# Up to two of three exponent-bit shifts moved to GpSimd, with term-wise products and a packed output projection, in a fused attention kernel

## The chip, the cores and the metric

The kernel runs on one core of a Trainium2 chip, with one launch. The metric is device time in microseconds (us). The kernel before takes 801.9 us at the median of its first three runs (798.03 to 802.26). Each timed run also has the mean clock that TensorE was granted, as a share of full speed.

## The reference, cut to what matters

Two attention layers read separate inputs of 2048 rows and 512 columns, and their outputs are joined side by side.

```python
def _A_ref(x, wq, wk, wv, wo):           # H = 32 query heads, ONE key/value head, Dh = 16
    q = (x @ wq).reshape(B, S, H, Dh).transpose(0, 2, 1, 3)
    k, v = x @ wk, x @ wv
    scores = einsum("bhqd,bkd->bhqk", q, k) * Dh ** -0.5
    p = softmax(scores)                   # 32 x 2048 x 2048 exponentials
    o = einsum("bhqk,bkd->bhqd", p, v)
    return o.transpose(0, 2, 1, 3).reshape(B, S, H * Dh) @ wo

def _B_ref(x, wqkv, w_phi, wo):           # linear attention
    ...
    phi_q = concat([softmax(pq), softmax(-pq)])     # the same for phi_k
    kv, z = einsum("bhsf,bhsd->bhfd", phi_k, v), phi_k.sum(s)
    o = (phi_q @ kv) / (phi_q . z + 1e-6)
    return o.reshape(B, S, D) @ wo
return concatenate([a, b], axis=-1)
```

Part A costs most: 32 x 2048 x 2048, or 134 million, exponentials. Part B is dense matrix work, small beside it.

## The kernel before

The program is planned when it is built. A small list scheduler in Python gives each job (a few instructions on one engine) an estimated duration and picks the order; the chip then runs that fixed order with semaphores.

**Scores on TensorE, a quarter of the array at a time.** A head has 16 columns, so a score matmul contracts over at most 32 rows. Four of them run side by side, each in its own group of 32 rows ("row tiles"). The products with the values use 32 columns each, four side by side ("column tiles").

```python
def score(self, pe, bank, sc, kap, g):            # row tile g
    return pe.matmul(self.ps[:, bank, :], lhsT=self.KR[32*g:32*g+32, ...], rhs=self.QA[32*g:32*g+32, ...],
                     start=True, stop=True, tile_position=(32 * g, 0))

def pv(self, q):                                  # ScalarE's path: four column tiles
    ...
    for g in range(4):
        mm = pe.matmul(ps[32*g:32*g+32, bank, :], lhsT=w, rhs=PT[:, slots[g], :], start=start, stop=stop,
                       tile_position=(0, 32 * g))
```

**Exponentials on two engines.** ScalarE takes three or two banks of scores at a time from PSUM (the memory that matmuls write) and writes exp. VectorE takes the other tiles ("quads" of four) by building the bits of a half-precision float: `bits` evicts a score tile from PSUM as an int16 that is roughly 1024·log2(e)·score plus a bias. The exponential is then a weighted sum of four such floats, whose bits are shifted by 0, 256, 512 and 768. The three shifts are VectorE additions of a constant. The weights sit in the matmul's stationary operand (`VK`).

```python
def bits():                                       # four times a quad
    v.tensor_scalar(out=Z[:, 0, h, :], in0=ps[:, bank, :], scalar1=Z1, scalar2=Z0, op0=mult, op1=add)
def shift(t):                                     # t = 1, 2, 3: three times a quad
    v.tensor_scalar(out=Z[:, t], in0=Z[:, 0], scalar1=256.0 * t, scalar2=None, op0=add)

def d_pv(self, quad):                             # one job of 16 column-tiled matmuls
    for k in range(4):
        for g in range(4):
            mm = pe.matmul(ps[32*g:32*g+32, bank, :], lhsT=w[:, k, :], rhs=Zf[:, k, sl[g], :], ...)
```

**Few banks.** PSUM has eight banks: three and two for ScalarE's score groups, one for the accumulator, and two that the bit path and all of part B share (`self.free = [6, 7]`). TensorE runs its instructions in order, so a job that lacks a bank stops everything behind it.

**Fillers.** The planner keeps a running weight of TensorE's recent work over 3.41 us and inserts matmuls with no use (`fill`) when there is a gap and the weight is under `ACTIVE`.

```python
def weight(self, j):
    if k == "fill": return (j.dur / 0.2133) * (0.512 if j.mode == "full" else 0.25)
    if j.mode == "row": return 0.28 * (self.gsize[j.name[1]] if k == "qk" else 1)
    if j.mode == "col": return 0.41 if k == "kv" else 0.68 if k == "pv" else 2.7
    return dict(qs=0.13, q4=0.4, s6=0.8, wf=0.4).get(k, 2.4 * (j.dur - 0.02))
...
    if n >= 2 and te > 14 and self.active(s) < self.ACTIVE:     # ACTIVE = 6.4
        ... issue a fill
```

**Output projection.** Each of 31 blocks is normalised on VectorE into `On` (12 slots). The projection uses eight matmuls for 128 rows, with the weights padded by zeros (`wo_pad`, 8 slots), since only 16 of every 32 rows carry data.

## Time and profile before

| | before |
|---|---|
| time, first three runs | 801.9 us (798.03 to 802.26) |
| span of the profiled run, its granted clock | 800.5 us, 0.981 |
| busy: TensorE, VectorE, ScalarE, GpSimd | 754.1, 727.9, 746.9, 17.2 us |
| ScalarE idle (span less busy) | 53.6 us |

The first fence has lines of the profile page of the kernel before: busy time by engine (share of the span, number of instructions); the granted clock in 40 slices (9 means 90% or more); the engines' shares of the chain of waits that ended last; and the costliest groups (line, engine, operation, tiles, count, then busy us and mean ns, then idle time just before and its main releaser).

```profile
PE 754.1 (94%) x7457; PEld 246.6 (31%) x7457; DVE 727.9 (91%) x1261; ACT 746.9 (93%) x688; POOL 17.2 (2%) x49
...
PEclk9999999999799999999999999999899999999999
...
DVE 64%; PE 26%; ACT 4%; DMA 3%; SPq 2%; issue 1%; POOL 0%; DVEq 0%; POOLq 0%
...
L1645 ACT ACTIVATE f_PT<-f_ps 128x1536 bf16<-128x1536 f32 x619 | 719.5, 1262 | 36.4 <-PE f_ps L1590 33.0
L1737 DVE TENSOR_SCALAR f_Z<-f_ps 128x512 int16<-128x512 f32 x500 | 326.6, 681 | 28.5 <-PE f_ps L1590 28.1
L1590 PE MATMUL f_ps<-f_QA,f_KR 32*128 32x512 bf16 x2048 | 314.4, 389 | 24.2 <-DVE f_Z L1737 13.5
L1750 DVE TENSOR_SCALAR f_Z<-f_Z 128x2048 int16<-128x2048 int16 x375 | 247.8, 684 | 1.1
```

Three engines are over 90% busy. The chain says that VectorE ends last most often: L1737 are the evictions (`bits`), L1750 the shifts. ScalarE waits only 33 us in all for scores. TensorE's share of busy time has to be read with care, because ends of matmuls are modelled.

The table of stretches shows (columns: us, then busy us and instruction count of each engine, granted clock, share of the DMA engines, GB/s):

```profile
200.00:224.00 24.00, 23.47 (x201) 6.39 (x200) 21.39 (x38) 20.83 (x20) 0.00 (x0) 0.79 0.09 6
...
300.00:500.00 200.00, 191.23 (x1975) 64.75 (x1974) 183.53 (x316) 196.03 (x188) 5.35 (x10) 1.00 0.12 11
```

### The profile page before, as it was taken

To read this page: it belongs to the slowest core of one execution; us is meant where nothing else is said; L and a number is where in the kernel's file an instruction comes from. 1 tells how busy PE (TensorE), PEld (TensorE's weight loads), DVE (VectorE), ACT (ScalarE), POOL (GpSimd) and SP (SyncE) were. 2 spreads that over 40 slices of the span, in tenths; PEclk is the share of its full clock that TensorE was granted. 3 is DMA by queue.
4 is the path that set the end of the run, shared out by engine and by line. 5 is a ranking of instruction groups with operands and counts; after the bars stand their busy time and mean duration, and the time that the engine had idled before them with its cause. 6 is when DMAs were issued, how large, how long until landed. Compare 5 with 4: busy or idle time off the path is not lost.

```text
span 800.5 us, 17448 instructions
## 1 busy us (share of the span) xinstructions
PE 754.1 (94%) x7457; PEld 246.6 (31%) x7457; DVE 727.9 (91%) x1261; ACT 746.9 (93%) x688; POOL 17.2 (2%) x49
## 2 busy tenths in 40 slices
PE   8999999999999999999999999999999999989995
PEld 2323222333233233333333333333223333333332
DVE  3799999999899999997989898999899989999954
ACT  3999998999899999999999999999899999999972
POOL 5000000000000000011000000000000000000000
PEclk9999999999799999999999999999899999999999
DMA  6561111110111110111101111110111111011111
GB/s 133 111 129 9 9 7 8 8 8 4 6 8 21 22 8 4 7 9 8 9 4 19 35 7 9 21 15 10 6 9 21 22 21 19 11 9 15 21 14 37
DMA packets 45181, 17.12 MB, mean 21 GB/s; under 512 B 37092, under 2 KB 43236, under 8 KB 45096
## 3 DMA queue, kind: packets, MB, share of 16 engines
q1 hardware_dynamic: 45096, 15.93, 16.0%
q8 instruction: 60, 0.98, 0.5%
q14 instruction: 25, 0.20, 0.1%
HBM read 2.15 MB, written 4.19 MB: 8 GB/s over the span
## 4 chain that ended last, share of the span: by engine, by line
DVE 64%; PE 26%; ACT 4%; DMA 3%; SPq 2%; issue 1%; POOL 0%; DVEq 0%; POOLq 0%
DVE f_Z L1737 26%; DVE f_Z L1750 19%; PE f_ps L1590 8%; PE f_ps L1775 4%; PE f_ps L1687 4%; ACT f_PT L1645 4%; PE f_ps L2084 3%; DVE f_vS L2033 2%; DVE f_ssum L2007 2%; PE f_ps L1396 2%; DVE f_On L1818 2%; DVE f_Wk L2144 2%; DVE f_accS L1402 2%; PE f_ps L1831 1%; DMA f_denS<-f_denS 1%
## 5 line engine op out<-in xcount | busy, mean ns | idle before, releaser
L1645 ACT ACTIVATE f_PT<-f_ps 128x1536 bf16<-128x1536 f32 x619 | 719.5, 1262 | 36.4 <-PE f_ps L1590 33.0
L1737 DVE TENSOR_SCALAR f_Z<-f_ps 128x512 int16<-128x512 f32 x500 | 326.6, 681 | 28.5 <-PE f_ps L1590 28.1
L1590 PE MATMUL f_ps<-f_QA,f_KR 32*128 32x512 bf16 x2048 | 314.4, 389 | 24.2 <-DVE f_Z L1737 13.5
L1750 DVE TENSOR_SCALAR f_Z<-f_Z 128x2048 int16<-128x2048 int16 x375 | 247.8, 684 | 1.1
L1590 PEld LDWEIGHTS f_ps<-f_QA,f_KR 32*128 32x128 bf16 x2048 | 80.1, 91 | 256.0 <-ACT f_PT L1645 87.9
L1687 PE MATMUL f_ps<-f_PT,f_VA 128*32 128x512 bf16 x1548 | 152.5, 393 | 0.7 <-DVE f_accS L1402 0.2
L1775 PE MATMUL f_ps<-f_Z,f_VK 128*32 128x512 f16 x2000 | 133.3, 387 | 3.7 <-DVE f_Z L1750 1.7
L1396 PE MATMUL f_ps<-f_ones,f_zero 128*128 128x512 bf16 (+9 forms) x229 | 65.9, 354 | 2.0 <-POOL f_zero L1415 1.3
L1687 PEld LDWEIGHTS f_ps<-f_PT,f_VA 128*32 128x32 bf16 x1548 | 38.1, 93 | 93.5 <-issue 82.7
L1775 PEld LDWEIGHTS f_ps<-f_Z,f_VK 128*32 128x32 bf16 x2000 | 42.9, 96 | 64.5 <-DVE f_Z L1750 14.3
L2084 PE MATMUL f_ps<-f_BxT,f_Wq 128*128 128x512 bf16 x128 | 33.2, 382 | 1.6 <-DVE f_Z L1737 1.0
L1396 PEld LDWEIGHTS f_ps<-f_ones,f_zero 128*128 128x128 bf16 (+2 forms) x229 | 17.7, 97 | 33.2 <-issue 21.7
L1831 PE MATMUL f_ps<-f_wo_pad,f_On 128*128 128x512 bf16 x96 | 24.9, 382 | 0.6 <-DVE f_Z L1737 0.6
L2144 DVE TENSOR_TENSOR f_Wk<-f_ps,f_wq 128x512 bf16<-128x512 f32 x32 | 21.7, 681 | 2.7 <-PE f_ps L2133 2.7
L1818 DVE TENSOR_TENSOR f_On<-f_accS,f_denS 128x512 bf16<-128x512 f32 x31 | 21.2, 682 | 1.3 <-DMA f_denS<-f_denS 1.2
L1402 DVE COPY f_accS<-f_ps 128x512 f32<-128x512 f32 x31 | 21.2, 684 | 1.1 <-PE f_ps L1687 1.0
L2091 ACT ACTIVATE f_ET<-f_ps 128x512 bf16<-128x512 f32 x32 | 20.8, 649 | 0.6 <-PE f_ps L2084 0.5
L1542 DVE TENSOR_SCALAR f_KR<-f_ps,f_half 128x512 bf16<-128x512 f32 x8 | 5.6, 746 | 15.8 <-PE f_ps L1534 15.8
L2033 DVE TENSOR_TENSOR f_vS<-f_ps,f_rs 128x1024 bf16<-128x1024 f32 x16 | 19.6, 1222 | 0.0
L2001 ACT ACTIVATE f_Ek<-f_ps 128x512 bf16<-128x512 f32 x32 | 17.7, 622 | 1.8 <-PE f_ps L1993 1.7
L2007 DVE TENSOR_REDUCE f_ssum<-f_Ek 128x64 f32<-128x1024 bf16 x16 | 19.4, 1212 | 0.0
L2174 PE MATMUL f_ps<-f_Bwo,f_oT 128*128 128x512 bf16 x64 | 16.6, 382 | 2.2 <-DVE f_Z L1737 1.2
(95 smaller groups left out, 325.9 us busy)
## 6 DMA issues: line engine op xcount, KB each, us to landing
f_denS<-f_denS SPq DMA_DIRECT2D x124, 30.0 KB, 3.0
out_dram<-f_outB SPq DMA_DIRECT2D x18, 128.0 KB, 1.9
f_denC<-f_accS SPq DMA_DIRECT2D x124, 2.0 KB, 1.7
f_denS<-f_denC SPq DMA_DIRECT2D x124, 2.0 KB, 1.7
out_dram<-f_outA SPq DMA_DIRECT2D x14, 128.0 KB, 2.2
f_wq<-in_A_wq_dram SPq DMA_DIRECT2D x1, 512.0 KB, 4.0
f_Bwv<-in_B_wqkv_dram SPq DMA_DIRECT2D x1, 512.0 KB, 5.3
f_Bwo<-in_B_wo_dram SPq DMA_DIRECT2D x1, 512.0 KB, 9.3
```

The lines of the kernel that those rows point to most:

```text
L1396: mm = pe.matmul(ps[0:m, bank, 0:n].rearrange("p (a n) -> p a n", n=128), lhsT=zero[0:r, 0:m], rhs=rhs, start=start, stop=start, **kw)
L1402: self.add("dve", lambda v: v.tensor_copy(out=out, in_=in_), reads=reads, writes=writes)
L1590: return pe.matmul(self.ps[:, bank, :], lhsT=self.KR[32 * g:32 * g + 32, sc % 2, kap * 128:(kap + 1) * 128], rhs=self.QA[32 * g:32 * g + 3 ...
L1645: self.add("act", lambda a: a.activation(out=PT[:, sl[0]:sl[0] + size, :], in_=ps[:, b0:b0 + size, :], func=ACT.Exp), reads=[("PS", b0 + i ...
L1687: mm = pe.matmul(ps[32 * g:32 * g + 32, bank, :], lhsT=w, rhs=PT[:, slots[g], :], start=start, stop=stop, tile_position=(0, 32 * g))
L1737: self.add("dve", lambda v: v.tensor_scalar(out=o, in0=ps[:, bank, :], scalar1=self.Z1, scalar2=self.Z0, op0=ALU.mult, op1=ALU.add), reads ...
L1750: self.add("dve", lambda v: v.tensor_scalar(out=Z[:, t], in0=Z[:, 0], scalar1=256.0 * t, scalar2=None, op0=ALU.add), reads=zk, writes=[("Z ...
L1775: mm = pe.matmul(ps[32 * g:32 * g + 32, bank, :], lhsT=w[:, k, :], rhs=Zf[:, k, sl[g], :], start=start and k == 0, stop=stop and k == 3, t ...
L1818: self.add("dve", lambda v: v.tensor_tensor(out=On[:, sc % 12, :], in0=accS[:, r, :], in1=R[:, r, :], op=ALU.mult), reads=[("accS", r), (" ...
L2033: self.add("dve", lambda v: v.tensor_tensor(out=vS[:, :, :, 0:16], in0=v3, in1=rs.unsqueeze(3).to_broadcast([128, 32, 2, 16]), op=ALU.mult ...
L2084: mm = pe.matmul(ps[:, bank, :], lhsT=w[:, dc].rearrange("p x h a f -> p (x h a f)")[:, G * 128:G * 128 + 128], rhs=xT[:, dc, m * 512:(m + ...
L2144: self.add("dve", lambda v: v.tensor_tensor(out=o, in0=i, in1=w.unsqueeze(3).to_broadcast([128, 2, 16, 16]), op=ALU.mult), reads=[("PS", b ...
```

## The change

The intent is to take VectorE off the chain:

- Of a quad's three shifts, up to two go to GpSimd, as int32 additions on pairs of int16 (1024 words). Each of the four bit patterns ("terms") has its own buffer of a ring of 12.
- Each term's four products become a job of their own, which can run as soon as its term is there.
- The planner models the port to SBUF (the on-chip memory) that VectorE and GpSimd share, for the shifts (`dS`) and the normalisations (`on`).
- The output projection is packed: two blocks share one `On` slot by small on-chip copies, so four matmuls do the work of eight. Part B's query features are computed once, and ScalarE takes exp of plus and minus with `scale`.
- Loads of part B that are needed late are issued later.

```diff
-    NQ = 3
+    NZ = 12
...
+        if j.eng == "pool" or j.name[0] in self.LOCK:
+            self.te_port = start + dur
...
+                    a, b = (Z[:, x].rearrange("p h n -> p (h n)").bitcast(I32) for x in (z0, z))
+                    c = self.step[:, t - 2, :].bitcast(I32).to_broadcast([128, 1024])
+                    fn = lambda g: g.tensor_tensor(out=b, in0=a, in1=c, op=ALU.add)
...
-        self.job(("dpv", quad), "pe", 0.87, lambda: self.d_pv(quad), mode="col", prio=1.4,
-                 after=[("dS", quad, t) for t in range(1, 4)] + [("va", x) for x in range(4)], ...)
+        for t in (3, 2, 1):
+            left = max(self.te["pool"] - self.fin, 0.0) + self.PSHIFT * self.pooled
+            eng = "pool" if t > 1 and left < self.PLEFT[3 - t] else "dve"
+            ...
+            self.job(("dS", quad, t), eng, 0.60 if eng == "dve" else self.PSHIFT, shift(t, eng), prio=2, ok=ok)
+        for t in range(4):
+            self.job(("dpv", quad, t), "pe", 0.22 if sc < 31 else 0.43, (lambda t: (lambda: self.d_pv(quad, t)))(t), mode="col", prio=1.4,
+                     after=([("dS", quad, t)] if t else []) + [("va", x) for x in range(4)], ok=lambda: self.acc_ok(sc))
...
-            for a in range(4 * half, 4 * half + 4):
-                mm = pe.matmul(ps[:, bank, :], lhsT=On[:, (8 * qc + a) % 12, q0:q0 + 128], rhs=self.wo_pad[:, a, :], start=(a == 0), stop=(a == 7))
+            for A in range(4):
+                mm = pe.matmul(ps[:, bank, :], lhsT=On[:, (4 * qc + A) % 6, q0:q0 + 128], rhs=self.wo_pad[:, A, :], start=(A == 0), stop=(A == 3))
...
-                job(("bq", m, G), "pe", 0.87, self.b_pq, ...)        # G in range(8)
+                job(("bq", m, G), "pe", 0.87, self.b_pq, ...)        # G in range(4)
...
+    PSHIFT = 1.95
+    PLEFT = (4.0, 2.0, 0.0)
+    LOCK = ("dS", "on")
```

By count, in the two programs' instruction order: VectorE shifts 375 → 177 and GpSimd shifts 0 → 228; VectorE evictions 500 → 540; exponential groups on ScalarE 619 → 603; changes between row, column and full tiling on TensorE, fillers left out, 1190 → 1340.

## The prediction

> **What bounds it now.** The profile page: span 800.5 us, ScalarE busy 746.9 (93%), VectorE 727.9 (91%), TensorE 754.1 (94%, modelled ends). In the table of stretches VectorE is 89 to 100% busy between 40 and 760 us, ScalarE 94 to 99%. The chain of waits that ended last is 64% VectorE, carried by two groups: the exponent-bit evictions from PSUM (500 x 681 ns) and three "add a constant" shifts per quad (375 x 684 ns). In the chain each takes 0.60 us of VectorE's time, since consecutive instructions overlap. ScalarE's exponentials (310 x 1474 ns, 309 x 1050 ns) are the other wall; it idles about 53 us, some 12 at the start, 10 at the end, the rest waiting for scores.
>
> **What the change moves**, by the instruction order of the two programs:
> - Shifts: VectorE 375 -> 177, GpSimd 0 -> 228; bit-path quads 125 -> 135. VectorE's evictions rise 500 -> 540; four scalings of Wq vanish. Net VectorE: -162 x 0.60 = about -97 us.
> - ScalarE: 8 three-bank and 8 two-bank exponentials fewer: 8 x (1.474 + 1.050) = -20 us.
> - TensorE: 64 fewer 512-column matmuls for the query features, 64 fewer in the output projection; 160 more column-tiled ones on the bit path, 40 fewer of ScalarE's. At about 0.22 us a full or four-way group: -28 + 9 - 2 = -21 us. But changes between row, column and full tiling grow from 1190 to 1340, as a quad's product is now issued term by term; this gives back perhaps 10 us.
> - SP queue: 60 small on-chip copies more; three part B transposes and the output weights leave the first 60 us. Nearly free: little waits on DMAs.
>
> **The port.** The Trainium skill, "SBUF — State Buffer", says VectorE and GpSimd share a port pair under an exclusive lock held for a whole instruction. Before, GpSimd works only at the start and for 6 us near 357 us, so no run yet shows it. "GPSIMD Engine Reference" (section 3.1) gives 2.6 cycles an element for two-input GpSimd ops: my estimate from that page for 1024 words is about 2.2 us, against 1.95 in the change's plan. So GpSimd holds the port 445 to 500 us; VectorE's 177 shifts and 31 normalisations (0.6 us each) need 125 more. That fits, but VectorE is in order: where real times drift from the plan, a VectorE shift stands behind up to 2 us of GpSimd. I expect 30 to 70 us of such stalls, inside the 97 us freed, so VectorE ceases to be the wall.
>
> **Critical path.** The gain is what the next walls allow: ScalarE's 747 - 20 = 727 us plus its waits, and TensorE, nearly full, 10 to 15 us lighter. Keeping ScalarE's idle time near 50 us gives 777.
>
> **Predicted: 776 us, 8 in 10 between 760 and 794. Faster by over 2%: 0.75; within 2%: 0.22; slower by over 2%: 0.03.**
>
> **What would show each step.**
> - VectorE busy 630 to 700 us; its share of the last chain well below 64%.
> - ScalarE busy 725 to 729 us, idle 45 to 60 us.
> - GpSimd shifts 1.9 to 2.4 us each, busy 440 to 550 us.
> - VectorE's remaining shifts longer than 684 ns where they overlap a GpSimd shift: that is the lock. Evictions from PSUM stay at 681 ns.
> - Fewer fill matmuls: TensorE has fewer gaps.
>
> **What would make it wrong.** GpSimd shifts over 2.6 us, or lock stalls above 100 us, which starve the score banks and idle ScalarE: then 790 to 820. The other way: before's ScalarE waits came mainly from VectorE releasing banks late; if they vanish, 760.

## More of the kernel before

**Part B is spread over part A.** `T_B = (54.0, 600.0)` gives the plan times between which its jobs are released, so that its dense matmuls fill TensorE beside the tiled ones.

**A check of range.** VectorE computes running maxima (`bmx` for part B's sums, others for q and k), and the last steps combine them in a flag; out of range, a slower general program runs. It does not run here.

The trace's clock records are only 1.0 or 0.5, and each but the last lasts a multiple of 3413 ns. The kernel before spends 26 us at half clock after its first 15 us, in five stretches.

## The result, and the profile after

The changed kernel takes **825.79 us** (median of four runs, 820.41 to 827.53); the kernel before takes 801.5 us. Ratios here are the mean time of one kernel's fast runs over that of the other's fast runs of the same rounds, so they are not quite the ratio of the medians quoted: **1.0301 (95% interval 1.0253 to 1.0348)**. The change makes the kernel 3% slower, outside the predicted range. Its outputs are correct.

| | before | after |
|---|---|---|
| span, granted clock of the profiled run | 800.5 us, 0.981 | 824.1 us, 0.928 |
| VectorE busy | 727.9 | 691.0 |
| ScalarE busy / idle | 746.9 / 53.6 | 731.9 / 92.2 |
| GpSimd busy | 17.2 | 473.2 |
| half-clock time after the first 15 us | 26 us, 5 stretches | 115 us, 13 stretches |

The same lines of the changed kernel's profile page:

```profile
PE 770.5 (93%) x7396; PEld 235.9 (29%) x7396; DVE 691.0 (84%) x1099; ACT 731.9 (89%) x672; POOL 473.2 (57%) x279
...
PEclk9999997999999999999999899999999997579678
...
PE 60%; DVE 29%; ACT 5%; DMA 2%; issue 1%; SPq 1%; POOL 1%; DVEq 0%; POOLq 0%
...
L1636 ACT ACTIVATE f_PT<-f_ps 128x1536 bf16<-128x1536 f32 x603 | 702.1, 1262 | 72.9 <-PE f_ps L1581 69.3
L1765 POOL TENSOR_TENSOR f_Z<-f_Z,f_step 128x1024 int32<-128x1024 int32 x228 | 459.5, 2016 | 318.8 <-DVE f_Z L1734 290.5
L1734 DVE TENSOR_SCALAR f_Z<-f_ps 128x512 int16<-128x512 f32 x540 | 352.3, 680 | 56.6 <-PE f_ps L1581 54.2
L1581 PE MATMUL f_ps<-f_QA,f_KR 32*128 32x512 bf16 x2048 | 336.3, 405 | 22.9 <-DVE f_Z L1734 11.4
L1760 DVE TENSOR_SCALAR f_Z<-f_Z 128x2048 int16<-128x2048 int16 x177 | 139.5, 811 | 4.7 <-PE f_ps L1796 3.3
```

VectorE did leave the chain (64% → 29%), and TensorE took its place (26% → 60%). ScalarE's exponentials wait 69.3 us for scores instead of 33.0. VectorE's evictions wait 54.2 us for scores instead of 28.1. Both consumers starve, and TensorE is what they starve for, although it has fewer full-array matmuls to do. Single evictions are as long as before (681 → 680 ns); the shifts that stayed on VectorE grew from 684 to 811 ns. Also new is the right end of the clock row, "7579678".

### Where the time went: two long stretches at half clock

Two of the 13 half-clock stretches are long: 37.5 us from 692.2 and 27.3 us from 767.3. Here is the table of stretches of the changed kernel, the two cold ones (at half clock), with a warm one (at full clock) between them:

```profile
core 0: us, PE busy (x) PEld busy (x) DVE busy (x) ACT busy (x) POOL busy (x), PEclk, DMA share, GB/s
...
692.00:729.00 37.00, 36.65 (x217) 6.60 (x218) 26.72 (x39) 24.71 (x22) 20.56 (x10) 0.50 0.12 7
735.00:763.00 28.00, 27.30 (x263) 8.03 (x263) 27.59 (x42) 27.91 (x26) 17.68 (x9) 1.00 0.10 8
767.00:794.00 27.00, 25.52 (x150) 5.28 (x150) 17.96 (x26) 19.15 (x16) 9.81 (x5) 0.51 0.11 8
```

The kernel before over the first of these stretches, in the same table:

```profile
692.00:729.00 37.00, 33.38 (x358) 11.73 (x354) 34.75 (x68) 35.20 (x32) 0.00 (x0) 1.00 0.15 10
```

In the first one the changed kernel's TensorE is "busy" for 36.65 of 37 us and runs only 217 matmuls, 5.9 a microsecond. In the warm stretch it runs 9.4, and the kernel before ran 358 in the same 37 us. ScalarE is busy for 24.71 us where it was busy for 35.20: 10 us of work are left undone in this stretch alone. Part B's dense work is over by then: in the changed kernel it ends between 650 and 690 us, in the kernel before near 790, so these stretches hold almost nothing but tiled matmuls and fillers.

### How a drop starts

The lumps come from waits like this one. The three timelines of the changed kernel between 178 and 185 us give start, duration, engine, line, operation and tiles; in brackets stands idle time just before and what ended it. First GpSimd, then VectorE, then TensorE:

```profile
178.79 4.19 POOL L1765 TENSOR_TENSOR f_Z<-f_Z,f_step 128x1024 int32<-128x1024 int32 x2 [0.37 <-DVE f_Z L1734]
```

```profile
177.42 1.29 DVE L1734 TENSOR_SCALAR f_Z<-f_ps 128x512 int16<-128x512 f32 x2 [0.33 <-PE f_ps L1581]
179.05 2.17 DVE L1864 TENSOR_TENSOR f_Ot<-f_accS,f_denS 128x512 bf16<-128x512 f32 x1 [0.34 <-DMA f_denS<-f_denS]
181.15 0.68 DVE L1406 CAST f_Wq<-f_ps 128x512 bf16<-128x512 f32 x1
```

```profile
179.70 0.39 PE L1581 MATMUL f_ps<-f_QA,f_KR 32*128 32x512 bf16 x2
181.89 0.39 PE L1581 MATMUL f_ps<-f_QA,f_KR 32*128 32x512 bf16 x1 [1.80 <-DVE f_Wq L1406]
182.20 0.40 PE L1678 MATMUL f_ps<-f_PT,f_VA 128*32 128x512 bf16 x4
```

A normalisation (L1864) starts at 179.05 while GpSimd shifts run. It takes 2.17 us where it took 0.68 in the kernel before. The cast behind it in VectorE's queue would free one of the two shared banks; it ends at 181.83. TensorE, in order, stands idle for 1.80 us until then. At 183.7 the clock record goes to 0.5.

This is not a single case. Leave out the last of the 13 half-clock stretches, at the program's end. Eight of the other twelve begin within 3 us of a VectorE instruction that stands beside a GpSimd shift and takes 1.5 to 2.4 us: `bmx` four times, a normalisation twice, a copy into `vS` once and a shift once. Before the other four no instruction is stretched that far. Between 20 and 690 us TensorE is idle for over 0.9 us at a time 11 times; in the kernel before, never.

I weighed all matmuls by window of 3.41 us, with weights like the planner's own (0.512 a full-array matmul of 512 columns, 0.28 a row tile, 0.17 a column tile; these weights are the kernel author's, not measured here). In the changed kernel, 190 windows stayed at full clock; all but five of them weigh over 5.0. The 13 windows just before a drop, leaving out the end of the program, weigh 1.8 to 4.9. Inside the long cold stretches the windows weigh 3.3 to 4.9, as TensorE did no more tiled work than that at half clock. A line near 5 is thus inferred from one trace, and it is a rough one: by the same weights one of the kernel before's drops followed a window of 5.7, and a window of 3.7 there stayed at full clock.

### The profile page after: what moved, and what is told of

Read it like the earlier page. It is cut to its first block, busy times and chain, and to the rows that moved or that the text cites. A ratio compares the mean times of both kernels' runs of the same rounds, so it can differ in the third digit from the quotient of the medians.

```text
span 824.1 us, 17611 instructions
## 1 busy us (share of the span) xinstructions
PE 770.5 (93%) x7396; PEld 235.9 (29%) x7396; DVE 691.0 (84%) x1099; ACT 731.9 (89%) x672; POOL 473.2 (57%) x279
## 4 chain that ended last, share of the span: by engine, by line
PE 60%; DVE 29%; ACT 5%; DMA 2%; issue 1%; SPq 1%; POOL 1%; DVEq 0%; POOLq 0%
PE f_ps L1581 21%; PE f_ps L1796 15%; DVE f_Z L1734 11%; PE f_ps L1678 9%; DVE f_Z L1760 5%; ACT f_PT L1636 4%; PE f_ps L1400 2%; PE f_ps L2129 2%; PE f_ps L2068 2%; PE f_ps L1571 2%; PE f_ps L1883 1%; DVE f_bmx L2058 1%; PE f_ps L2221 1%; DVE f_accS L1406 1%; DVE f_ssum L2052 1%
## 5 line engine op out<-in xcount | busy, mean ns | idle before, releaser
L1636 ACT ACTIVATE f_PT<-f_ps 128x1536 bf16<-128x1536 f32 x603 | 702.1, 1262 | 72.9 <-PE f_ps L1581 69.3
L1765 POOL TENSOR_TENSOR f_Z<-f_Z,f_step 128x1024 int32<-128x1024 int32 x228 | 459.5, 2016 | 318.8 <-DVE f_Z L1734 290.5
L1734 DVE TENSOR_SCALAR f_Z<-f_ps 128x512 int16<-128x512 f32 x540 | 352.3, 680 | 56.6 <-PE f_ps L1581 54.2
L1581 PE MATMUL f_ps<-f_QA,f_KR 32*128 32x512 bf16 x2048 | 336.3, 405 | 22.9 <-DVE f_Z L1734 11.4
L1796 PE MATMUL f_ps<-f_Z,f_VK 128*32 128x512 f16 x2160 | 198.1, 405 | 11.1 <-DVE f_accS L1406 5.9
L1760 DVE TENSOR_SCALAR f_Z<-f_Z 128x2048 int16<-128x2048 int16 x177 | 139.5, 811 | 4.7 <-PE f_ps L1796 3.3
L1400 PE MATMUL f_ps<-f_ones,f_zero 128*128 128x512 bf16 (+9 forms) x172 | 53.6, 376 | 1.9 <-POOL f_zero L1419 1.3
L2068 PE MATMUL f_ps<-f_Bwv,f_BxT 128*128 128x512 bf16 x64 | 18.5, 416 | 2.2 <-DVE f_Z L1734 2.2
L1571 PE MATMUL f_ps<-f_AxT,f_wq 128*128 128x512 bf16 x64 | 19.1, 428 | 1.1 <-DVE f_Z L1734 1.1
L2038 PE MATMUL f_ps<-f_Wk,f_BxT 128*128 128x512 bf16 x64 | 17.4, 397 | 2.1 <-DVE f_Z L1734 2.1
```

The source lines that it names most:

```text
L1400: mm = pe.matmul(ps[0:m, bank, 0:n].rearrange("p (a n) -> p a n", n=128), lhsT=zero[0:r, 0:m], rhs=rhs, start=start, stop=start, **kw)
L1571: mm = pe.matmul(ps[:, bank, :], lhsT=self.wq[:, dc, A * 128:A * 128 + 128], rhs=xT[:, dc, qc * 512:(qc + 1) * 512], start=(dc == 0), stop ...
L1581: return pe.matmul(self.ps[:, bank, :], lhsT=self.KR[32 * g:32 * g + 32, sc % 2, kap * 128:(kap + 1) * 128], rhs=self.QA[32 * g:32 * g + 3 ...
L1636: self.add("act", lambda a: a.activation(out=PT[:, sl[0]:sl[0] + size, :], in_=ps[:, b0:b0 + size, :], func=ACT.Exp), reads=[("PS", b0 + i ...
L1734: self.add("dve", lambda v: v.tensor_scalar(out=o, in0=ps[:, bank, :], scalar1=self.Z1, scalar2=self.Z0, op0=ALU.mult, op1=ALU.add), reads ...
L1760: fn = lambda v: v.tensor_scalar(out=Z[:, z], in0=Z[:, z0], scalar1=256.0 * t, scalar2=None, op0=ALU.add)
```

## The experiments

Two theories were to be told apart:

1. **The lock.** GpSimd's shifts hold a port that VectorE's instructions need; VectorE stops in lumps of 1 to 2 us; banks come free late; TensorE idles; its clock falls.
2. **The rest of the change.** Less full-array work, part B ending early, and products issued term by term leave TensorE's stream thinner, and its clock falls without any lock.

The expectations also name a theory 3: term-wise issue, by its extra changes of tiling, slows TensorE even at a clock that holds.

Fourteen kernels were run. All give correct outputs but one, which is a measurement by itself. "Clock" is the granted clock of a run. A run counts as slow when it is over 1.5% above the fastest of its kernel. The medians and ranges quoted use all runs. The profiled run of three kernels was a slow one: all shifts on VectorE, the lock holders, and the products grouped again.

### All shifts on VectorE, the rest of the change kept

```diff
-    PLEFT = (4.0, 2.0, 0.0)
+    PLEFT = (0.0, 0.0, 0.0)
```

> The changed kernel with all three shifts of a quad on VectorE: packed projections, term-wise products and late part B loads stay, GpSimd has no part in the stream. Theory 1 (the port lock stalls VectorE in lumps of 1 to 2 us, TensorE starves in them and its clock is halved): shifts back at 680 to 690 ns, mean granted clock 0.97 or more, 795 to 808 us. Theory 2 (128 fewer full-array matmuls and fewer fills take away the activity that keeps the clock up, lock or no lock): clock 0.95 or less, over 810 us. Theory 3 (term-wise issue with 150 more tiling changes slows TensorE itself): over 810 us at a clock of 0.97 or more.

Measured: 817.26 us (806.58 to 823.21), ratio 1.0165 (1.0087 to 1.0243). The clocks are 0.946 (a run counted as slow), 0.956, 0.957 and 0.973. In the profiled run, the slow one, shifts are back at 683 ns, and the half-clock time is 89 us in 12 stretches.

What follows: without any GpSimd shift the clock is still lost, so theory 1 is not the whole story. The changed kernel's own 825.79 us is only 1% above this, with much more work taken off VectorE. Neither theory alone fits.

### The same, with GpSimd additions whose results nobody uses

Every engine but GpSimd runs the same instructions in the same order as in the run above; 242 additions on a scratch buffer are added.

```diff
+        x = self.scr.rearrange("p h n -> p (h n)").bitcast(I32)
+        for t in (3, 2):
+            c = self.step[:, t - 2, :].bitcast(I32).to_broadcast([128, 1024])
+            self.S.add("pool", ... g.tensor_tensor(out=x, in0=x, in1=c, op=ALU.add), writes=["scr"], deps=[the quad's evictions])
```

> The kernel all_dve with the same instructions in the same order on every other engine, plus 242 GpSimd adds of the same shape on a scratch tile that nobody reads, started where the changed kernel would start its shifts. No data passes between GpSimd and the others, so anything that slows comes from the shared port. Theory 1: VectorE's shifts rise from about 685 to over 800 ns and the sum of squares of exponentials' maximum step (two SBUF inputs, 64 columns) from 220 to over 500 ns; clock falls by 0.02 or more against all_dve; 15 to 60 us slower than all_dve. Theories 2 and 3: within 5 us of all_dve.

(The "exponentials' maximum step" there means the running maximum of part B's sums, `bmx`.)

Measured: 1163.53 us (1157.61 to 1167.34), ratio 1.4551. The clock is 0.747 to 0.753. Two groups of this run, with idle time and its releasers last:

```profile
L1762 DVE TENSOR_SCALAR f_Z<-f_Z 128x2048 int16<-128x2048 int16 x363 | 491.4, 1390 | 3.6 <-PE f_ps L1803 2.6
L1736 DVE TENSOR_SCALAR f_Z<-f_ps 128x512 int16<-128x512 f32 x484 | 317.2, 681 | 80.4 <-PE f_ps L1583 76.4
```

What follows: the lock is shown by itself. Shifts go from 683 to 1390 ns (363 of them, 257 us together), normalisations from 682 to 934 and 958, `bmx` from 214 to 295 (over 500 was expected). Evictions from PSUM stay at 681. The loss of 346 us is larger than the lengthening of these groups, and far beyond the 15 to 60 us expected: in this order a quad's shifts come due just when its GpSimd additions do, and with the stalls the clock falls to 0.75.

### Part B stretched to a later end

```diff
-    T_B = (54.0, 600.0)
+    T_B = (54.0, 680.0)
```

> The changed kernel with the release times of part B's jobs spread to 680 instead of 600 us, so that its full-array matmuls reach into the last 100 us. If the two long half-clock stretches of the changed kernel near the end (37 and 27 us) last because no full-array work is left to raise the activity, they shrink to under 20 us in all, mean clock rises to 0.945 or more, and 10 to 25 us are won: 800 to 815 us. If those stretches come from stalls alone, they stay and the time is within 5 us of the changed kernel.

Measured: 803.4 us (796.19 to 810.76), ratio 1.0011 (0.9923 to 1.0098), clocks 0.959, 0.969, 0.942 (slow) and 0.946. From 690 us to the end, half-clock time falls from 70 to 18 us, of which 6 and 8 us lie at the very end. The table of stretches of this kernel, over the same time as the first cold stretch above and as the warm one behind it:

```profile
692.00:729.00 37.00, 35.09 (x330) 11.66 (x330) 33.12 (x61) 32.07 (x29) 22.90 (x12) 0.87 0.11 12
735.00:763.00 28.00, 27.52 (x256) 8.50 (x248) 25.88 (x43) 27.69 (x25) 24.32 (x12) 1.00 0.13 16
```

What follows: the expectation was met. Leaving some dense work for the end wins 22 us with one number, and nothing else about the lock or the shifts was touched. The long cold stretches were that part of the loss. Other edits below end them too, so dense work at the end is not shown to be the only way.

### Fillers in every gap

```diff
-    ACTIVE = 6.4
+    ACTIVE = 99
```

> The changed kernel with the planner's ceiling on activity for filler matmuls taken away, so that every planned TensorE gap is filled (about 5 us more filler). Theory 2: the clock comes back to 0.96 or more and the time falls to 800 us or less. Theory 1: the gaps that matter are not in the plan, so few fillers stand there; clock rises by under 0.02 and the time stays within 10 us of the changed kernel, 812 to 830 us.

Measured: 809.51 us (806.65 to 810.77), ratio 1.0101 (1.0059 to 1.0142), clocks 0.956 to 0.965. What follows: 32 more fillers (204 instead of 172), and the order that they bring, win 16 us against the changed kernel, as the clock rises from 0.928 to about 0.96. This lies between the two theories' numbers. Fillers only go into gaps that the plan sees, and lock stalls outside the planner's model are not among them.

### The dense work put back, as plain repeats

The packed projections and the query features are done twice, into the same bank: 112 full-array matmuls more, about 24 us of TensorE time at 0.22 us each.

```diff
+            job(("opx", qt), "pe", 0.87, (lambda qt: (lambda: self.outproj(qt)))(qt), mode="full", prio=0.9, after=[("op", qt)])
...
+                job(("bqx", m, G), "pe", 0.87, self.b_pq, after=[("bq", m, G)], mode="full", prio=0.9)
```

> The changed kernel with the work that packing saved done again for nothing: each of the 12 output-projection groups and 16 query-feature groups runs twice into the same bank, 112 more full-array matmuls, about 24 us more of TensorE work. If the lost full-array activity is what lets the clock fall (theory 2), the mean clock rises from 0.93 to 0.95 or more and the time does not rise in spite of the extra work: 808 to 826 us. If TensorE time is what binds (theory 3), or only the port stalls count (theory 1), the work is simply added: 832 to 850 us at a clock under 0.945.

Measured: 812.73 us (809.01 to 817.19), ratio 1.0152 (1.0099 to 1.0205), clocks 0.954 to 0.968. What follows: a kernel that does 24 us more of TensorE work, to no use, is 13 us *faster*. Work as such was not the limit; the clock moved the time. Theory 2's number was hit: dense work can hold the clock up. That it was the removed matmuls which had held it up is less sure, because the repeats change the order of the plan too, and up to 690 us the half-clock time is the same 44 us as in the changed kernel; only the tail is better (15 us instead of 70). It is not all of the loss, as the time stays 1.5% above the kernel before.

### The same repeats, with all shifts on VectorE

```diff
-    PLEFT = (4.0, 2.0, 0.0)
+    PLEFT = (0.0, 0.0, 0.0)      # beside the repeats of the run above
```

> The same give-back on the version with all shifts on VectorE (817 us at a mean clock of 0.958). Theory 2: clock 0.97 or more, 800 to 815 us, so no slower. Theory 3: 828 to 845 us at a clock of 0.96 or less.

Measured: 817.21 us (811.53 to 822.65), ratio 1.0175 (1.0122 to 1.0228), clocks 0.963 to 0.979. What follows: against the all-VectorE kernel (817.26) the 24 us of extra work cost nothing and bring nothing in time, though the clocks are a little higher. Theory 2's number (800 to 815 us) was narrowly missed. So the repeats pay for themselves in clock, here just so. It does not restore the kernel before, which also has its shifts on VectorE; something else in the change costs about 1.7% when GpSimd does not repay it.

### The missed lock holders modelled too

The planner of the changed kernel knows that shifts and normalisations want the port. It does not know of three part B steps: `rs` (with `bmx`), `vs` and `qw`.

```diff
-    LOCK = ("dS", "on")
+    LOCK = ("dS", "on", "rs", "vs", "qw")
```

> The changed kernel whose planner also counts the other VectorE steps that were seen to stretch beside a GpSimd shift (running maximum of the sums of exponentials, the copy of the reciprocals, the query normalisation) as users of the shared port. If unplanned port conflicts start the drops of the clock (theory 1), the running maximum falls from 890 to under 400 ns, the clock rises to 0.945 or more, and the time falls to 802 to 816 us. If they are not what matters, 820 to 832 us.

Measured: 805.07 us (793.1 to 807.88), ratio 0.9968 (0.988 to 1.0057), clocks 0.952 to 0.979. Two of the four runs, the profiled one among them, count as slow; the fast ones took 804.42 and 793.1 us. The `bmx` group and the small copy into `vS`, of the changed kernel and then of this one, in the list of groups:

```profile
L2058 DVE TENSOR_TENSOR f_bmx<-f_ssum,f_bmx 128x64 f32<-128x64 f32 x16 | 14.2, 890 | 0.0
L1406 DVE CAST f_vS<-f_rs 128x64 bf16<-128x64 f32 x16 | 9.4, 586 | 0.0
```

```profile
L2058 DVE TENSOR_TENSOR f_bmx<-f_ssum,f_bmx 128x64 f32<-128x64 f32 x16 | 3.7, 230 | 0.0
L1406 DVE CAST f_vS<-f_rs 128x64 bf16<-128x64 f32 x16 | 9.5, 592 | 0.0
```

What follows: theory 1's number was hit. But the edit kept only `bmx` out of GpSimd's holds: the copy into `vS`, which belongs to `vs`, still takes 592 ns (313 in the kernel before). The median falls by 21 us, of which `bmx` accounts for 10.5 (16 x 0.66). TensorE's gaps of over 0.9 us between 20 and 690 us fall from 11 to 4, so the lock's stalls do reach TensorE. Yet in the profiled run the half-clock time up to 690 us does not fall (58 us against 44); the tail alone is better. That a stall costs more than its own length is likely, but this run does not show it.

### Three remedies together

```diff
-    LOCK = ("dS", "on")
+    LOCK = ("dS", "on", "rs", "vs", "qw")
-    T_B = (54.0, 600.0)
-    ACTIVE = 6.4
+    T_B = (54.0, 680.0)
+    ACTIVE = 99
```

> Three remedies at once on the changed kernel: part B spread to 680 us, fillers in every planned gap, and the longer list of port users. If stalls and lost activity together made the loss, the clock comes to 0.965 or more and the time to 782 to 798 us, below both kernels. If they do not add up, 798 to 812 us.

Measured: **791.01 us** (788.94 to 793.57), ratio **0.9875 (0.9838 to 0.9911)**, clocks 0.969 to 0.978. ScalarE's exponentials wait 34.1 us for scores, as in the kernel before (33.0), with ScalarE busy for 733.6 us. Half-clock time is 35 us. What follows: with the clock back, the change is worth having, by about 1.2%. The expectation was met. It still gets less than the 25 us that were predicted.

### TensorE's clock by itself

A kernel with nothing but TensorE streams on constant data, back to back; wrong outputs. After some full-array matmuls it runs tiled streams of 4 row tiles and 4 column tiles, of 3 and 4, and of 1 and 4. Each is entered warm first, then after an idle gap of 7 to 8.5 us.

```python
MIX = lambda pe, r, c, n: [(row(pe, r), col(pe, c))[1] for _ in range(n)][-1]
stages = [(0, FULL 100), (0, MIX 4,4), (0, FULL 60), (0, MIX 3,4), (0, FULL 60), (0, MIX 1,4),
          (1, MIX 4,4), (1, MIX 3,4), (1, MIX 1,4), (1, FULL 100)]      # 1: an idle gap first
```

> A kernel that only measures TensorE's clock; its outputs are zeros and wrong on purpose. Streams of full-array matmuls, and of row-tiled (4, 3 or 1 tiles) and column-tiled (4 tiles) matmuls in turn, each tiled stream once entered at full clock and once after an idle gap of some 7 us. If tiled work alone holds a fast clock but cannot regain it, the mixes with 3 or 1 row tiles run at full clock after full-array work and stay at half clock after the gap, while the full-array stream regains it within two 3.4 us windows. If tiled work is as good as full-array work, all streams are at full clock from the second window on; if it is not enough even to hold, the mixes fall to half clock both ways.

Measured: one run, 356.3 us. The table of stretches (us, TensorE busy and matmuls, weight loads, ScalarE, GpSimd, then the clock): tiled streams entered warm (three rows), then 4+4, 3+4 and 1+4 after a gap.

```profile
33.00:66.00 33.00, 32.90 (x400) 10.26 (x402) 0.00 (x0) 0.00 (x0) 1.00 0.01 1
80.00:112.00 32.00, 31.84 (x341) 9.78 (x339) 0.00 (x0) 0.00 (x0) 1.00 0.01 2
126.00:147.00 21.00, 21.00 (x165) 6.25 (x165) 0.00 (x0) 0.00 (x0) 1.00 0.00 1
...
171.00:196.00 25.00, 25.00 (x308) 7.71 (x304) 0.00 (x0) 0.00 (x0) 1.00 0.01 1
216.00:260.00 44.00, 44.00 (x287) 8.77 (x283) 0.00 (x0) 0.00 (x0) 0.50 0.00 1
272.00:324.00 52.00, 51.15 (x239) 9.86 (x235) 0.79 (x1) 0.00 (x0) 0.50 0.00 1
```

What follows: this is the sharpest result. The same gapless stream of 3 + 4 tiles runs at full clock when it is entered at full clock, and at half clock for its whole length when it is entered cold. It does not lift itself out: the clock stays at half for 129.7 us in one piece, through the 3 + 4 and the 1 + 4 stream and the gap between them, until full-array matmuls come (at 335 us the clock is 1.00 again). The 4 + 4 stream, just a little denser, is back at full clock 5 us after it starts (165.5 to 170.5 us). So this stream has two states that last, and which one it is in depends on history: its 50 pairs take about 54 us cold and 33 us warm. That the same happens from 692 us on in the changed kernel is an inference: the gap there is only 1.16 us, and the two stretches do end, after 37.5 and 27.3 us.

The run also shows a cost of changing the tiling. Groups of four alternating between row and column tiles start every 0.327 us at full clock:

```profile
33.01 0.40 PE L27 MATMUL ps<-x,w 32*128 32x512 bf16 x4
33.34 0.40 PE L33 MATMUL ps<-x,w 128*32 128x512 bf16 x4
33.67 0.40 PE L27 MATMUL ps<-x,w 32*128 32x512 bf16 x4
```

In the kernel before, by its TensorE timeline, a group of 16 column-tiled matmuls started at 99.81 us and the next group at 100.79. If that 0.98 us holds one change and four steps of four, then a change costs about 0.11 us (0.327 − x and 0.98 − 4x are equal for x = 0.22 us). With 150 more changes that is about 16 us of TensorE time, called an estimate.

### The products grouped again, in the changed kernel

A quad's 16 products are one job again, waiting for all four terms; all else is as in the changed kernel.

```diff
-        for t in range(4):
-            self.job(("dpv", quad, t), "pe", 0.22 if sc < 31 else 0.43, (lambda t: (lambda: self.d_pv(quad, t)))(t), mode="col", prio=1.4,
-                     after=([("dS", quad, t)] if t else []) + [("va", x) for x in range(4)], ok=lambda: self.acc_ok(sc))
+        self.job(("dpv", quad, 0), "pe", 0.87 if sc < 31 else 1.72, lambda: [self.d_pv(quad, t) for t in range(4)], mode="col", prio=1.4,
+                 after=[("dS", quad, t) for t in (1, 2, 3)] + [("va", x) for x in range(4)], ok=lambda: self.acc_ok(sc))
```

> The changed kernel with a quad's four term products issued as one group of 16 again, after all its shifts. Theory 3 (term-wise issue costs TensorE through more tiling changes): 800 to 815 us. Theories 1 and 2: the drops of the clock come from stalls and from lacking full-array work, neither of which this touches; 815 to 832 us, clock under 0.95, or better only as far as the larger number of planned fillers (44 instead of 32 us) lifts the clock.

Measured: 792.99 us (791.65 to 807.21, five runs), ratio 0.989 (0.9866 to 0.9913), clocks 0.941 (slow), then 0.965 to 0.969. Tiling changes fall from 1340 to 1117, and the plan has 223 fillers instead of 172. The first line of the profiled run's page, the slow one:

```profile
PE 742.5 (92%) x7373; PEld 242.7 (30%) x7435; DVE 668.6 (83%) x1092; ACT 730.6 (91%) x674; POOL 471.6 (59%) x279
```

What follows: this edit wins 33 us at the median, and beats the kernel before by 1.1%. The 51 fillers more that came with it are a rival which the expectation had named and no run takes apart. TensorE's busy time, 742.5 us against 770.5, cannot be compared: this trace has 7373 matmuls for 7435 weight loads, so 62 matmuls are missing from it. The fast runs beat the kernel before at a lower clock (0.967) than its own (0.981), so more than clock was won; that TensorE's stream became shorter is likely, and not shown.

### The three remedies, with all shifts on VectorE

```diff
-    PLEFT = (4.0, 2.0, 0.0)
+    PLEFT = (0.0, 0.0, 0.0)       # beside later part B and ACTIVE = 99
```

> The combined version (791 us) with all shifts back on VectorE and nothing on GpSimd: what GpSimd is worth once the clock is held. If the relief of VectorE is worth something at a held clock, this is slower: 797 to 808 us at a clock of 0.97 or more. If GpSimd brings nothing, 786 to 794 us.

Measured: 815.6 us (811.45 to 823.46), ratio 1.0193 (1.0121 to 1.0264), clocks 0.954 to 0.972. What follows: with the same end of part B and fillers, moving shifts to GpSimd is worth about 25 us (815.6 − 791.0, runs of different rounds). The clocks are a little lower here, so a part of this may be clock, and the time is above the expected 797 to 808 us. So the central idea of the change does gain, when the clock is nearly held. (With no shift on GpSimd the longer lock list has nothing to keep apart.) Beside it, it shows that the rest of the change without GpSimd is a loss.

### Fillers in every gap, in the kernel before

```diff
-    ACTIVE = 6.4
+    ACTIVE = 99
```

> Control: the kernel before with the ceiling on fillers taken away, as in the combined version. If the 10 us that the combined version gains come from fillers alone, this gains them too: 788 to 794 us. If the kernel before has no clock to regain (0.983 as it is), it stays within 5 us: 796 to 806 us.

Measured: 809.81 us (803.55 to 812.97), ratio 1.0092 (1.0034 to 1.0149), clocks 0.970 to 0.979. What follows: the gain of the combined version is not merely a gain that the old kernel had left lying. There fillers cost about 1%, a little more than either expectation had allowed. The later end of part B, the other remedy, was not tried in the kernel before.

### Term-wise products alone, in the kernel before

```diff
-        self.job(("dpv", quad), "pe", 0.87, lambda: self.d_pv(quad), mode="col", prio=1.4, after=[all three shifts])
+        for t in range(4):
+            self.job(("dpv", quad, t), "pe", 0.22 if sc < 31 else 0.43, (lambda t: (lambda: self.d_pv(quad, t)))(t), mode="col", prio=1.4,
+                     after=([("dS", quad, t)] if t else [the four evictions]) + [("va", x) for x in range(4)], ok=lambda: self.acc_ok(sc))
```

> The kernel before with one part of the change alone: each of a quad's four term products is issued as its own group of four, as soon as its shift is done; all shifts stay on VectorE, nothing is packed. Changes of tiling rise from 1190 to 1424. If term-wise issue is itself a main cause (each extra change costs about 0.11 us of TensorE, and thinner work lets the clock fall), 812 to 830 us at a clock under 0.97. If it only hurts together with the port stalls, 800 to 808 us.

Measured: 804.41 us (800.05 to 809.46), ratio 1.0043 (0.9969 to 1.0116), clocks 0.975 to 0.990, with 1424 tiling changes. What follows: by itself, term-wise issue costs nothing that is clear of zero. It is not *the* cause. In the changed kernel undoing it wins 33 us; that stalls and missing dense work had used up a reserve there is the likely reason, and not shown.

Two comparisons lie in this run. The kernel with all shifts on VectorE has the packing, the ring of buffers and the late loads besides. It takes 13 us more (817.26 us, in other rounds) at a lower clock (0.946 to 0.973), with no GpSimd shift in either: the rest of the change seems to cost clock without any lock. And part B's dense work ends at 668 us here, as early as in the changed kernel, yet only 5 us after 690 us are at half clock. An early end of part B alone does not make the long stretches.

### Grouped products and the later part B together

```diff
     # the grouped d_pv of above, and
-    T_B = (54.0, 600.0)
+    T_B = (54.0, 680.0)
```

> The changed kernel with the grouped products of quadwise (793 us) and part B spread to 680 us. If the two remedies add, 776 to 788 us at a clock of 0.97 or more, which is what had been predicted for the change. If both only hold the same clock, 788 to 798 us.

Measured: 808.82 us (802.28 to 810.78), ratio 1.0049 (0.9972 to 1.0127), clocks 0.934 to 0.944; 107 us at half clock in 13 stretches. What follows: this missed its expectation plainly. Two remedies that won 33 and 22 us alone win 17 us together. The clock fell, so what was gained in work was lost in cold windows. Every edit gives the planner another order, and with it, it seems, other windows fall short. Why this order has so many is not settled.

## Why the prediction was wrong

What held, against the profile after:

- VectorE busy 691.0 us (630 to 700 predicted), its share of the chain 29% where it had been 64%.
- The port lock. "I expect 30 to 70 us of such stalls": adding each lengthened group of the changed kernel against the kernel before gives 22.5 us for the shifts (177 x 0.127), 10.7 for `bmx` (16 x 0.668), 4.9 for `Ot` (15 x 0.328), 4.4 for a small copy into `vS` (16 x 0.273) and 1.9 for `On`: 44 us. Evictions from PSUM did not change (681 and 680 ns). The Trainium skill, "SBUF — State Buffer", section "Who interferes with whom", says that an instruction of two SBUF inputs contends with a GpSimd instruction that reads SBUF; the trace agrees, with `bmx` going from 222 to 890 ns. The prediction had named only shifts and normalisations; a third of the stalls came from part B's small instructions, `bmx` and the copy into `vS`.
- GpSimd shifts of 1.9 to 2.4 us: 2016 ns at the mean, 1.89 us when alone. Busy 473.2 us (440 to 550 predicted).

What failed:

- **The step "inside the 97 us freed, so VectorE ceases to be the wall", as if that made the stalls harmless.** The sum was right and the use of the sum was wrong. The stalls come in lumps of 1 to 2 us on an in-order engine, and only two shared banks lie between it and TensorE. At 179 us a 2.17 us normalisation gave a TensorE gap of 1.80 us, and 1.8 us after its end came the half clock. Total slack on VectorE does not help a stall in the one instruction that frees a bank. The prediction's own warning was 790 to 820 us with stalls of over 100 us; the time went past that with 44 us of them.
- **The step "TensorE, nearly full, 10 to 15 us lighter".** The prediction counted removed full-array matmuls as pure gain, at about 0.22 us each. They also helped to keep TensorE at full clock, which fell from 0.981 to 0.928. The clock was nowhere in the prediction, although the profile before showed it: 0.79 between 200 and 224 us. Putting the dense work back as idle repeats *gained* 13 us.
- **"Fewer fill matmuls: TensorE has fewer gaps."** There were fewer (172 against 229), but not because TensorE had fewer gaps: those over 0.9 us between 20 and 690 us rose from none to 11. Many came from locks that the plan did not model, where no filler stood.
- **"This gives back perhaps 10 us" for term-wise issue.** The tiling changes alone are near that (an estimate of 16 us, above). But grouping them again, with the fillers that came along, is worth 33 us in the changed kernel, and term-wise issue costs nothing clear of zero in the kernel before, for 234 changes more. A cost that depends so much on the rest of the kernel can't be carried as a fixed term of a sum.
- **ScalarE idle 45 to 60 us:** it was 92.2 us, of which 69.3 in waits for scores. This is where the sum broke: ScalarE's work was nearly as predicted (731.9 us, against 725 to 729), and what was slow was TensorE, in gaps and at half clock.

How much the clock explains: runs of one and the same kernel differ in clock and in time. Among fast runs, from 0.959 to 0.979 the kernel with the longer lock list goes from 804.42 to 793.1 us; from 0.956 to 0.973 the all-VectorE kernel goes from 816.53 to 806.58; from 0.946 to 0.969 the one with the later part B from 806.55 to 796.19. That is 4.5 to 5.9 us for each 0.01. The changed kernel's fall from 0.981 to 0.928 is then worth about 24 to 31 us. At the clock of the kernel before it would take some 795 to 802 us. That is an estimate from the spread within kernels, and it assumes that the clock is the cause and not a mere companion; the gate run and the run with repeats speak for it. It leaves a second, smaller error: even then the gain would be 0 to 7 us and not 25. The best version measured gains about 10.

Where the single remedies gained is in their profiles. Half-clock time up to 690 us and after it, in us (stretches that begin in the first 15 us left out):

| kernel | to 690 us | after 690 us |
|---|---|---|
| before | 24 | 3 |
| changed | 44 | 70 |
| later part B | 48 | 18 |
| fillers in every gap | 58 | 14 |
| repeats | 44 | 15 |
| longer lock list (a slow run) | 58 | 12 |
| products grouped (a slow run) | 75 | 20 |
| three remedies together | 20 | 14 |

None of the five single edits has less half-clock time up to 690 us than the changed kernel; only the three together do. All lack its two long stretches, though they aim at different causes. The part before 690 us costs too: by then the kernel before had started 1808 of its 2048 score matmuls, the changed one 1774, the one with the longer lock list 1780. So a rival stands: any other order of the plan might have missed the trigger at 692 us. No kernel was run with its order changed and nothing else, and the single gains are not proof of their theories.

Why the tail chose 692 us: VectorE's calculation of the flag (six small instructions, 689.4 to 691.4, no lock involved) let TensorE idle for 1.16 us, and no dense work was left to lift the clock again. The first and the last of the six, and TensorE's next matmul, in the timelines:

```profile
689.42 1.04 DVE L1955 TENSOR_REDUCE f_mrow<-f_Bwv 1x4 f32<-1x512 f32 x1
691.28 0.14 DVE L1962 TENSOR_SCALAR flag<-f_mrow 1x1 int32<-1x1 f32 x1
692.08 0.48 PE L1581 MATMUL f_ps<-f_QA,f_KR 32*128 32x512 bf16 x1 [1.16 <-DVE f_Z L1734]
```

In the kernel before the same six left a gap of 1.01 us before 718.9 us; four full-array matmuls of part B came next, and the clock stayed at full. The kernel with the longer lock list has no dense work from 690 us to the last 25 us either; there the flag left 0.64 us, and no long stretch followed. So these three traces speak for a trigger and a lack of dense work together. The second long stretch began 3 us after a shift that stood 2.42 us beside GpSimd.

What stays open:

- The shares of lock stalls, removed dense work and term-wise issue in the 24 us. All of their remedies ended the same two stretches, so the single gains (21 us for the lock list, 13 for the repeats, 33 for the grouping, 22 for the later part B) do not add, as the last run shows.
- Whether a mere change of order would have won as much.
- The exact rule of the clock gate. The weights used here are the planner's.
- Why grouping and the later part B together leave the clock at 0.94.

## What to carry to other kernels

When TensorE runs mostly tiled matmuls, its clock is a resource to budget like time: read the granted clock and the matmuls per microsecond of each stretch, not the busy share, and before removing dense matmuls or fillers as "pure gain" ask what the remaining stream looks like in its worst 3.4 us. When work moves to GpSimd, list *every* VectorE instruction that shares the port, small ones too, and ask of each how long TensorE can go on while it stands still, because a stall that delays the freeing of a bank can cost more than its own length. If a change loses against a clean sum, first run it with dummy dense work added: a kernel that becomes faster by doing more is not short of time for its work. And before you credit a remedy, look where in the run it gained: here five of them, meant for different causes, ended the same two stretches.

## What the Trainium skill lacked or had wrong

- "TensorE: Matmul & The Clock Gate", "Part 1: The HAM clock gate": it gives a window of 3413 ns and, for this gate, only half or full clock, and records agree (0.5 and 1.0, in multiples of 3413 ns). It has the clock fall after an idle window and rise after a busy one. Here gaps of 1.1 to 2.4 us among tiled matmuls came just before nine of the twelve drops, and before the other three no gap was over 0.6 us.
- The same page lacks that a tiled stream without any gap can stay at half clock: a stream of 3 row tiles and 4 column tiles held full clock when entered warm (80 to 112 us) and half clock when entered cold (216 to 260 us, TensorE busy for 44.00 of 44 us); full clock came back with full-array matmuls.
- The same page, "A second HAM failure mode: psum-queue depth-cycling", says that frequent short idling between groups makes the clock swing. That agrees with the changed kernel (13 stretches, 115 us), and it is the passage that the prediction should have used.
- "TensorEngine Tiling (Array Packing)", "Tiling Modes", says that changing the mode drains TensorE, and gives no cost. Worked out here: about 0.11 us at full clock (groups of four start every 0.327 us when alternating).
- "SBUF — State Buffer", "Who interferes with whom": it agrees, but beyond two ratios (6.8 and 1.5 times) it gives no sizes. VectorE's 683 ns shift became 1390 ns beside steady GpSimd additions, and a 222 ns instruction of 64 columns became 890 ns.
- "GPSIMD Engine Reference", section 3.1: about 2.6 cycles an element for two inputs gave an estimate of 2.2 us for 1024 words. An undisturbed one took 1.89 us here, where the second input is a broadcast word. The measurement decides.
